# Duo attention with a leaky MoE layer: chunk 0's q in three loads of single tokens, its sinks on GpSimd

## The chip, the core and the metric

The kernel runs on one core of one Trainium2 chip. The metric is the device time of one execution in microseconds (us); the median of five runs counts. The engines are TensorE (PE, with its weight loads as PEld), VectorE (DVE), ScalarE (ACT), GpSimd (POOL) and SyncE (SP). GpSimd, SyncE and ScalarE also issue DMAs, each from its own queue. Only DMAs issued by GpSimd turn float32 into bfloat16 on the way here.

## What is computed

```python
# q, k, v: (4 batches, 8 heads, 768 tokens, 64); heads 0, 2, 6 are "retrieval" heads
scores = q @ k^T / sqrt(64)
causal = rel >= 0                       # rel = query position - key position
stream = causal & (key < 4 | rel < 64)  # 4 sink tokens and a window of 64
a = softmax(where(retrieval head, causal, stream))
x = (a @ v) as (3072 tokens, 512)
h = x @ w_in                            # (512, 2048)
out = max(0.01 * h, h) @ w_out          # (2048, 512), float32 out
```

## The kernel before

**Chunks.** The 3072 tokens are eight chunks of 384 (`CH`): two for each batch, so chunk 0 is the first half of batch 0. Each chunk goes through a preparation (q and k transposed so that the 64 dimensions lie on partitions: tiles `qts` and `kt`), attention (scores, exponential, attention times values into `po`, division, transposition into `xt`), the first layer (`in_slots`, L562, with the leaky function on ScalarE or VectorE) and the second (`out_slots`, L602). The order of every engine's work is written out by hand (`manual_schedule`), the functions return lists of slots that `merge`, `spaced` and `run` interleave, so that the layers of chunk n run beside the attention of chunk n + 1. An instruction waits only for what it needs, but each engine takes its instructions in the order of the program.

**Loads.** GpSimd issues all loads of q, v and the weights and all of k but chunk 0's (`load`, L82; `load_w`, L99). A load of one tensor for one chunk is three DMAs, one for each group `g` of 128 tokens; partition p of group g holds token 128 g + p. At most eight of GpSimd's DMAs are under way; the ninth waits for the first to land. Chunk 0 is the exception: `load_k0` (L70) brings its k as float32 through SyncE in two halves of four heads, and `load_q0` (L78) brings its q in one DMA. Both use the pattern `h (p g) d -> p h (g d)`: partition p holds the tokens 3p, 3p + 1, 3p + 2, so that a piece of three tokens (768 bytes) is contiguous in memory. What comes out of the transposes has then to be put in order of tokens, which `tok` (L331) does by scattered writes.

**The start.** In the program's order:
- GpSimd: the issue for q (L80), `ident` (a memset and a select in masks.py), `m_caus` (L153, L133), three issues for v of chunk 0, w_in parts 0 and 1, then k, q and v of chunk 1, w_in parts 2 and 3, w_out in four parts, and four memsets of `kz`.
- VectorE: memsets of `idle` (what the warm-up matmuls read), `sv`, the ones' column of `va`, `shift`, the zeros in `kt` (L138, L139), `ksink`, two of the five `ats` tiles (L666); `m_h`, a mask of heads, from `ident` (L167, L171).
- ScalarE: five small loads into `sv` (the sink tokens' values), a table load, the other three `ats` tiles (L669).
- `prep_first` (L308): VectorE casts heads 0 to 3 of k (L312), ScalarE heads 4 to 7 (L313). TensorE transposes k in two halves (L324, into banks `pt` and `py`), and between and behind them runs warm-up matmuls, then transposes q (L329) with 24 transposes of 64 columns into two `po` banks. VectorE moves the first half of k into `kt` (L341), makes a mask (L178, L179), and moves the first half of q (L355); ScalarE makes masks (L174, L175), moves the second half of k (L339) and of q (L357).
- Attention of chunk 0: `a0` is a list of slots, each with scores of one group of keys (L416 for retrieval heads, L458 for the others), one slot for the sinks (L396, which reads `ksink` and all of q), and the attention-value matmuls (L383) four slots later. The first four slots need only heads 0 and 2, that is the first half of q. After these four VectorE writes the sink keys out of `kt` into `ksink` (`sink_keys`, two copies, L238), the sink values out of `sv` and `m_h` into `vs` (`sink_values`, L187 and L189), and two 64-column blocks of `ident` into `shift` (`shifts`, L161 and L162). `v_shift_pe` (L218) then multiplies `va` by `shift` on TensorE to get values moved by 64 tokens into `vb` (L224, L227).

`sink_keys` and `sink_values` are also used for later batches, on VectorE; this the change leaves as it is.

Of the kernel before, what the change touches and what calls it, by code (L numbers as in the profile page):

```python
# [12 lines left out]
BF16 = mybir.dt.bfloat16  # L13
ACTF = mybir.ActivationFunctionType
ALU = mybir.AluOpType

IS_RETR = [1, 0, 1, 0, 0, 0, 1, 0]
CH = 384
# [3 lines left out]
def kernel(  # L22
# [12 lines left out]
    nc = tc.nc  # L35
    B, H, S, D = q.shape
    assert (B, H, S, D) == (4, 8, 768, 64)
    NS = int(n_sink)
# [12 lines left out]
    one = ctx.enter_context(tc.tile_pool(name="one", bufs=1))  # L51
# [5 lines left out]
    def bank(tag, shape, dtype):  # L57
        return ps.tile(shape, dtype, name=tag, tag=tag, bufs=BANKS[tag])


    kw, qw = (t[0, :, 0:CH].rearrange("h (p g) d -> p h (g d)", g=3) for t in (k, q))
    nat = {nm: ap.rearrange("b h (c g p) d -> b c p h g d", g=3, p=128) for nm, ap in (("q", q), ("k", k), ("v", v))}
    w_in_r = moe_w_in.rearrange("(g p) n -> p g n", p=128)
    w_out_r = moe_w_out.rearrange("(g p) n -> p g n", p=128)
# [3 lines left out]
    cast = {}  # L68

    def load_k0(half):  # L70
# [3 lines left out]
            cast["k", 0] = rot.tile([128, 3, H, D], BF16, name="kb", tag="kb", bufs=2)  # L74
        hs = slice(4 * half, 4 * half + 4)
        nc.sync.dma_start(out=stage["k"][:, hs], in_=kw[:, hs])

    def load_q0():  # L78
        cast["q", 0] = one.tile([128, H, 3 * D], BF16, name="q0")
        nc.gpsimd.dma_start(out=cast["q", 0][:], in_=qw)  # L80

    def load(n, nms="kqv"):  # L82

        b, c = divmod(n, 2)
        for nm in nms:
            if nm == "k" and n >= BY_DMA:

                for g in range(3):
                    for hh in range(2):
                        nc.gpsimd.dma_start(out=kz[n % 2][:, g, hh::2, D * hh : D * hh + D],  # L90
                                            in_=nat[nm][b, c, :, hh::2, g])
                continue
            if nm != "v":
                cast[nm, n] = rot.tile([128, 3, H, D], BF16, name=f"{nm}b", tag=f"{nm}b", bufs=2)
            for g in range(3):
                o = va[b % 2][:, 3 * c + g, :, 0:D] if nm == "v" else cast[nm, n][:, g]
                nc.gpsimd.dma_start(out=o, in_=nat[nm][b, c, :, :, g])  # L97

    def load_w(which, i):  # L99

        if which == "in":
            c = slice(512 * i, 512 * i + 512)
            nc.gpsimd.dma_start(out=w_in_bf[:, :, c], in_=w_in_r[:, :, c])
        else:
            c = slice(4 * i, 4 * i + 4)
            nc.gpsimd.dma_start(out=w_out_bf[:, c, :], in_=w_out_r[:, c, :])
# [5 lines left out]
    def bf(name, *shape):  # L112
        return one.tile([128, *shape], BF16, name=name)

    ident = bf("ident", 128)
# [3 lines left out]
    kt = [bf(f"kt{i}", 4, 2, S) for i in range(2)]  # L119
    va = [bf(f"va{i}", 6, H, D + 1) for i in range(2)]  # L120
    vb = [bf(f"vb{i}", 5, H, D + 1) for i in range(2)]
    vs = [bf(f"vs{i}", H, D + 1) for i in range(2)]

    sv = one.tile([128, B, D], FP32, name="sv")
# [21 lines left out]
    m_h = bf("m_h", H)  # L146
# [9 lines left out]
    def spread(ap, n, w):  # L156
        return ap.rearrange("p (o r) -> p o r", o=1).to_broadcast([128, n, w])

    def shifts():

        nc.vector.tensor_copy(shift[:, 0, 0:64], ident[:, 64:128])  # L161
        nc.vector.tensor_copy(shift[:, 1, 64:128], ident[:, 0:64])  # L162

    def masks_sinks():

        with nc.allow_low_precision("one term of each sum is not zero"):
            nc.vector.tensor_reduce(m_h[:], ident[:, 0 : NS * H].rearrange("p (h r) -> p h r", r=NS),  # L167
                                    axis=mybir.AxisListType.X, op=ALU.add)
        for h in range(H):
            if IS_RETR[h]:  # L170
                nc.vector.memset(m_h[:, h : h + 1], 0.0)  # L171
# [11 lines left out]
        nc.vector.tensor_copy(m_win0[:, 0, :], m_caus[:, 0:64])  # L183
        nc.vector.memset(m_win0[0:NS, 1, :], 1.0)

    def sink_values(b):
        nc.vector.tensor_copy(vs[b % 2][:, :, D], m_h[:])  # L187
        m = m_h[:, 1:H].rearrange("p (h o) -> p h o", o=1).to_broadcast([128, H - 1, D])
        nc.vector.tensor_tensor(vs[b % 2][:, 1:H, 0:D], spread(sv[:, b, :], H - 1, D), m, op=ALU.mult)  # L189


    idle = {}
# [1 line left out]
    def warm_up(n, w=128):  # L194
        if not idle:
            idle["s"] = bf("idle", 512)
            nc.vector.memset(idle["s"][:], 0.0)
            idle["d"] = bank("psS", [128, 512], FP32)
        for _ in range(n):
            nc.tensor.matmul(idle["d"][:, 0:w], lhsT=idle["s"][:, 0:128], rhs=idle["s"][:, 0:w], start=True, stop=True)  # L200
# [7 lines left out]
    qts = {}  # L208
# [17 lines left out]
            src = p[:, 0:w].rearrange("p (h d) -> p h d", h=7)  # L226
            nc.vector.tensor_copy(vb[0][:, t, 1:H, :], src)  # L227

    def sink_keys(n):
        b, c = divmod(n, 2)  # L230
        if c:
            return
        for hh in range(2):
            r = slice(64 * hh, 64 * hh + 64)
            d = ksink[b % 2].rearrange("p (a c) -> p a c", a=4)[r, :, NS * hh : NS * hh + NS]
            st = [p for p in range(4) if not IS_RETR[2 * p + hh]]
            for ps2 in [slice(0, 4)] if len(st) == 4 else [slice(p, p + 1) for p in st]:
                nc.vector.tensor_copy(d[:, ps2], kt[b % 2][r, ps2, hh, 0:NS])  # L238

    def prep_pair(n, p, tag="pt", eng=("v", "v", "v")):  # L240
        b, c = divmod(n, 2)
# [66 lines left out]
    def prep_first():  # L308

        k0 = stage["k"].rearrange("p h (g d) -> p g h d", g=3)  # L310
        qts[0] = rot.tile([128, 4, CH], BF16, name="qt", tag="qt", bufs=3)
        nc.vector.tensor_copy(cast["k", 0][:, :, 0:4], k0[:, :, 0:4])  # L312
        nc.scalar.activation(out=cast["k", 0][:, :, 4:8], in_=k0[:, :, 4:8], func=ACTF.Copy)  # L313
        pts = {}
        for nm, half, tag in (("k", 0, "pt"), ("k", 1, "py"), ("q", 0, "po"), ("q", 1, "po")):
            pt = pts[nm, half] = bank(tag, [128, 2, 4, 128], BF16)
            if nm == "q":
                continue
            if half == 1:
                warm_up(9)  # L320
            for e in range(2):
                p = 2 * half + e
                for g in range(3):
                    nc.tensor.transpose(pt[:, e, g, :], cast[nm, 0][:, g, 2 * p : 2 * p + 2, :], ident[:])  # L324
        warm_up(8)
        for p in range(4):
            for g in range(3):
                for hh in range(2):
                    nc.tensor.transpose(pts["q", p // 2][64 * hh : 64 * hh + 64, p % 2, g, :],  # L329
                                        cast["q", 0][:, 2 * p + hh, D * g : D * g + D], ident[:])  # L330
        tok = lambda ap: ap.rearrange("p e (t g) -> p e t g", g=3)  # L331

        def k_rows(half, hh, act=False):
            ps2 = slice(2 * half, 2 * half + 2)
            r = slice(64 * hh, 64 * hh + 64)
            src = pts["k", half][r, :, 0:3, :].rearrange("p e g t -> p e t g")
            dst = tok(kt[0][r, ps2, hh, 0:CH])
            if act:
                nc.scalar.activation(out=dst, in_=src, func=ACTF.Copy)  # L339
            else:  # L340
                nc.vector.tensor_copy(dst, src)  # L341

        def q_rows(half):
            return (tok(qts[0][:, 2 * half : 2 * half + 2, :]),
                    pts["q", half][:, :, 0:3, :].rearrange("p e g t -> p e t g"))

        nc.vector.tensor_sub(m_w[:], m_caus[:, 64:128], m_caus[:, 0:64])
        negative_causal()
        k_rows(0, 0)
        k_rows(0, 1)  # L350
        k_rows(1, 0, True)
        k_rows(1, 1, True)
        negative_window()
        d, r = q_rows(0)
        nc.vector.tensor_copy(d, r)  # L355
        d, r = q_rows(1)
        nc.scalar.activation(out=d, in_=r, func=ACTF.Copy)  # L357

# [262 lines left out]
    def run(*lists):  # L621
        for l in lists:
            for f in l:
                f()
# [16 lines left out]
        return [lambda p=p: prep_pair(n, p) for p in range(4)]  # L641


    load_q0()
    make_identity(nc, ident)
    warm_up(9, 512)
    nc.vector.memset(sv[:], 0.0)
# [9 lines left out]
    load(0, "v")  # L657
    load_w("in", 0)
    load_w("in", 1)
    load(1, "kq")  # L660
    load(1, "v")
    load_w("in", 2)
    load_w("in", 3)
    for j, a in enumerate(ats):
        if j < 2:
            nc.vector.memset(a[:, :, 1:3, :], 0.0)  # L666
        else:
            z = idle["s"][:, 0:CH].rearrange("p (a e t) -> p a e t", a=3, e=2)
            nc.scalar.activation(out=a[:, :, 1:3, :], in_=z, func=ACTF.Copy)  # L669
    masks_sinks()  # L670
    for i in range(4):
        load_w("out", i)
    for t in kz:
        nc.gpsimd.memset(t[:, :, 0::2, D:], 0.0)
        nc.gpsimd.memset(t[:, :, 1::2, 0:D], 0.0)
    prep_first()
    A0 = Attention(0, ("psS", "ph"), po_tags=("po", "po", "py", "po"))
    a0 = A0.slots(order=[0, 2, 1, 3, 4, 5, 6, 7], lag=lambda t: 4, XLAG=None, sink_after={0, 2})
    warm_up(8)
    run(a0[0:4])  # L680
    sink_keys(0)
    sink_values(0)
    shifts()
    run(a0[4:6])
    v_shift_pe()
    run(a0[6:14])
    i0 = in_first(0, ("ph", "psS", "ph", "psS"))
# [36 lines left out]
    m = merge(out0[5:] + out_slots(1, ("ph", "py", "ph")), a2)  # L724
# [63 lines left out]
```

## Time and profile before

| what | us |
|---|---|
| median of five runs (lowest, highest) | 237.37 (236.95, 237.73) |
| the profiled execution | 237.08 |
| its span, first to last instruction | 235.4 |
| TensorE busy | 227.9 (97%) |
| ScalarE busy | 129.3 (55%) |
| VectorE busy | 89.7 (38%) |
| GpSimd busy | 77.8 (33%) |
| granted TensorE clock, mean | 0.998 |
| first score matmul (L416) | 9.76 after the span's start |

The profile is of one execution on the chip. Its page gives busy time by engine, the span in 40 slices, the chain of waits that ended last, and groups of instructions by source line. Each row of the chain names a start, a length, and what took that time: an engine with tile and line, or "issue" where the engine waited for nothing that the profile shows. In the timeline a row is a start, the time from there to the end of the last of `xcount` instructions, engine, line and tiles (output <- input); in brackets stands idle time ahead of it and what ended that. The last columns of a row of groups are busy time and mean ns of one, then idle time ahead. Matmuls are pipelined, so one that shows 0.3 us may be followed by the next after half of that. For DMAs the profile has packets by queue (the software queue is the one that GpSimd fills) and the time from an issue to its landing.

### The profile page before, as it was taken

The page shows a single profiled execution, that of the slowest core. Times are in us where ns is not written, and L with a number is a line of the kernel's source. Part 1 is how long each engine was busy: PE and PEld are TensorE (multiplying, and loading weights), DVE is VectorE, ACT ScalarE, POOL GpSimd, SP SyncE. Part 2 cuts the span into 40 slices and gives each one's busy share as a digit, 9 for nine tenths or more (in the row PEclk, how much of TensorE's full clock was granted, in tenths as well). Part 3 has the DMA queues.
Part 4 walks back from the last instruction along what each step waited for, and adds up shares of the span by engine and source line. Part 5 has one row for each costly group of instructions (what it writes and reads, how often), then busy time and mean ns, then how long its engine had stood idle before and what let it go on. Part 6 is the DMA issues. An engine that isn't in the chain of part 4 may idle for free.

```text
span 235.4 us, 5134 instructions
## 1 busy us (share of the span) xinstructions
PE 227.9 (97%) x2064; PEld 138.9 (59%) x2064; DVE 89.7 (38%) x244; ACT 129.3 (55%) x282; POOL 77.8 (33%) x102
## 2 busy tenths in 40 slices
PE   7899899999999999999999999999999999999994
PEld 2786566556664676666546665566556665555553
DVE  7875479208662254144212351344213341111121
ACT  4977775661540798666357763556366763333300
POOL 7938942879762274372049100000000000000000
PEclk9999999999999999999999999999999999999999
DMA  7999999999999999999999998495210221111112
GB/s 168 178 180 163 220 222 186 155 124 167 143 162 223 166 189 159 158 115 169 150 199 178 128 140 150 111 137 154 72 45 0 65 58 40 45 45 45 47 45 89
DMA packets 110699, 30.54 MB, mean 130 GB/s; under 512 B 101460, under 2 KB 106836, under 8 KB 110676
## 3 DMA queue, kind: packets, MB, share of 16 engines
q0 software_dynamic: 74144, 13.24, 76.9%
q1 hardware_dynamic: 36432, 16.95, 39.0%
q8 instruction: 16, 0.26, 0.5%
q14 instruction: 7, 0.06, 0.1%
q10 hardware_dynamic: 100, 0.02, 0.0%
HBM read 27.28 MB, written 6.29 MB: 143 GB/s over the span
## 4 chain that ended last, share of the span: by engine, by line
PE 86%; DVE 5%; DMA 4%; ACT 3%; issue 1%; ACTq 0%
PE ph L562 26%; PE py L602 14%; PE pt L602 10%; PE po L383 7%; PE psS L562 6%; PE ph L602 4%; PE psS L416 4%; PE psS L602 4%; DMA xt<-xs 4%; PE psS L458 2%; ACT at L425 2%; PE po L602 1%; PE psS L396 1%; PE ph L416 1%; DVE kt L341 1%
## 5 line engine op out<-in xcount | busy, mean ns | idle before, releaser
L562 PE MATMUL ph<-xt,w_in_bf 128*128 128x384 bf16 x416 | 85.7, 326 | 0.6 <-DMA xt<-xs 0.5
L570 ACT ACTIVATE g<-ph 128x384 bf16<-128x384 f32 x102 | 50.1, 491 | 51.6 <-PE ph L562 51.2
L562 PEld LDWEIGHTS <-w_in_bf 128*128 128x128 bf16 x512 | 46.5, 98 | 31.4 <-issue 0.5
L602 PEld LDWEIGHTS <-g 128*128 128x128 bf16 x400 | 35.8, 98 | 26.3
L602 PE MATMUL py<-w_out_bf,g 128*128 128x512 bf16 (+1 forms) x176 | 44.6, 369 | 0.0
L425 ACT ACTIVATE at<-psS 128x384 bf16<-128x384 f32 x66 | 32.4, 495 | 11.6 <-PE psS L416 10.2
L90 POOL DMA_DIRECT2D kz<-in_k_dram x30 | 22.4, 766 | 29.6 <-DVE kz L736 12.3
L602 PE MATMUL pt<-w_out_bf,g 128*128 128x512 bf16 x112 | 30.2, 379 | 0.0
L97 POOL DMA_DIRECT2D va<-in_v_dram x24 | 21.2, 898 | 9.8 <-DMA w_in_bf<-in_moe_w_in_dram 3.6
L97 POOL DMA_DIRECT2D qb<-in_q_dram x21 | 18.7, 906 | 10.9 <-DMA va<-in_v_dram 4.9
L416 PE MATMUL psS<-qt,kt 128*128 128x384 bf16 (+2 forms) x86 | 21.5, 288 | 0.2
L562 PE MATMUL psS<-xt,w_in_bf 128*128 128x384 bf16 x96 | 20.5, 326 | 0.0
L383 PE MATMUL po<-va,at 128*128 128x65 bf16 x237 | 19.5, 193 | 0.2 <-DVE at L433 0.2
L383 PEld LDWEIGHTS <-at 128*128 128x128 bf16 x252 | 15.9, 98 | 5.6 <-issue 0.6
L466 ACT ACTIVATE ats<-psS 128x384 bf16<-128x384 f32 x32 | 15.8, 492 | 4.9 <-PE psS L458 4.3
L607 DVE COPY o<-py 128x512 f32<-128x512 f32 (+1 forms) x11 | 7.3, 664 | 28.1 <-PE py L602 28.1
L501 DVE TENSOR_TENSOR xs<-po,linv 128x384 bf16<-128x384 f32 x30 | 16.7, 557 | 1.0
L416 PEld LDWEIGHTS <-kt 128*128 128x128 bf16 x108 | 10.2, 97 | 8.7 <-issue 1.5
L458 PEld LDWEIGHTS <-kt 128*128 128x128 bf16 x240 | 11.8, 98 | 5.5 <-issue 0.2
L433 DVE TENSOR_TENSOR at<-at,m_caus 128x128 bf16<-128x128 bf16 x21 | 4.7, 224 | 26.0 <-ACT at L425 25.9
L383 PEld LDWEIGHTS <-ats 128*128 128x128 bf16 x240 | 11.4, 97 | 3.8 <-DVE ats L476 0.6
L570 ACT ACTIVATE g<-psS 128x384 bf16<-128x384 f32 x22 | 10.8, 491 | 4.7 <-PE psS L562 4.7
(135 smaller groups left out, 243.2 us busy)
## 6 DMA issues: line engine op xcount, KB each, us to landing
out_dram<-o SPq DMA_DIRECT2D x23, 256.0 KB, 2.9
va<-in_v_dram POOLq DMA_DIRECT2D x24, 128.0 KB, 10.9
qb<-in_q_dram POOLq DMA_DIRECT2D x21, 128.0 KB, 10.7
w_in_bf<-in_moe_w_in_dram POOLq DMA_DIRECT2D x4, 512.0 KB, 9.2
w_out_bf<-in_moe_w_out_dram POOLq DMA_DIRECT2D x4, 512.0 KB, 14.7
kz<-in_k_dram POOLq DMA_DIRECT2D x30, 64.0 KB, 7.8
vb<-va SPq DMA_DIRECT2D x8, 195.0 KB, 6.5
vb<-va SPq DMA_DIRECT2D x6, 130.0 KB, 8.3
```

The costliest lines, as they stand in the source:

```text
L90: nc.gpsimd.dma_start(out=kz[n % 2][:, g, hh::2, D * hh : D * hh + D], in_=nat[nm][b, c, :, hh::2, g])
L97: nc.gpsimd.dma_start(out=o, in_=nat[nm][b, c, :, :, g])
L383: nc.tensor.matmul(o, lhsT=lhsT, rhs=rhs, start=first, stop=False, skip_group_check=True)
L416: nc.tensor.matmul(s[:, off : off + w], lhsT=kt[i][:, p, hh, 128 * kj : 128 * kj + 128], rhs=qts[n][:, p, lo:CH], start=(j == 0), stop=(j ...
L425: nc.scalar.activation(out=a[:, 0:off], in_=s[:, 0:off], func=ACTF.Exp, scale=SM)
L458: nc.tensor.matmul(s[:, 64 * m : 64 * m + 64], lhsT=kt[i][:, p, hh, k0 : k0 + 128], rhs=qts[n][:, p, 64 * m : 64 * m + 64], start=(m == 0) ...
L466: nc.scalar.activation(out=av_, in_=s[:, 0:CH].rearrange("p (j e f) -> p j e f", j=3, e=2), func=ACTF.Exp, scale=SM)
L501: nc.vector.tensor_tensor(xs[:], po[:, :, :, 0:D], linv.to_broadcast([128, 3, 2, D]), op=ALU.mult)
L562: nc.tensor.matmul(ph[:, 0:CH], lhsT=w_in_bf[:, g, 128 * t : 128 * t + 128], rhs=xts[n][:, g, :], start=(g == 0), stop=(g == KG - 1))
L570: nc.scalar.activation(out=gs[n][:, t, :], in_=ph[:, 0:CH], func=ACTF.Prelu, alpha=0.01)
L602: nc.tensor.matmul(py[n][:, 0 : c1 - c0], lhsT=gs[n][:, ng, 128 * tt : 128 * tt + 128], rhs=w_out_bf[:, ng, c0:c1], start=(ng == 0), stop= ...
L607: nc.vector.tensor_copy(o[:, 0 : c1 - c0], py[n][:, 0 : c1 - c0])
```

## The change

Chunk 0's q is loaded as every other chunk's: three DMAs of 128 tokens each, one token and head (256 bytes) to a piece, into a tile `qb`. q's tokens are then in their natural order after the transposes, which are 12 of 128 columns, grouped by g with two warm-up matmuls ahead of the second and the third group; the moves into `qts` write contiguously. k of chunk 0 stays in its interleaved order.

The sink keys and values of chunk 0 are written by GpSimd instead of VectorE. In GpSimd's order they stand behind the issues of v of chunk 0 and w_in parts 0 and 1, and ahead of all loads of chunk 1. The keys' copies wait for `kt`, which VectorE and ScalarE write; the values' product waits for the loads into `sv`. `shifts` moves ahead of `prep_first`, so on VectorE ahead of the cast of k. A third `ats` tile is zeroed by VectorE, so ScalarE zeroes two.

```diff
-    def load_q0():
-        cast["q", 0] = one.tile([128, H, 3 * D], BF16, name="q0")
-        nc.gpsimd.dma_start(out=cast["q", 0][:], in_=qw)
...
-    def sink_values(b):
-        nc.vector.tensor_copy(vs[b % 2][:, :, D], m_h[:])
+    def sink_values(b, eng=None):
+        eng = eng or nc.vector
+        eng.tensor_copy(vs[b % 2][:, :, D], m_h[:])
         m = m_h[:, 1:H].rearrange("p (h o) -> p h o", o=1).to_broadcast([128, H - 1, D])
-        nc.vector.tensor_tensor(vs[b % 2][:, 1:H, 0:D], spread(sv[:, b, :], H - 1, D), m, op=ALU.mult)
+        eng.tensor_tensor(vs[b % 2][:, 1:H, 0:D], spread(sv[:, b, :], H - 1, D), m, op=ALU.mult)
...
-    def sink_keys(n):
+    def sink_keys(n, eng=None):
...
-                nc.vector.tensor_copy(d[:, ps2], kt[b % 2][r, ps2, hh, 0:NS])
+                (eng or nc.vector).tensor_copy(d[:, ps2], kt[b % 2][r, ps2, hh, 0:NS])
...
         warm_up(8)
-        for p in range(4):
-            for g in range(3):
-                for hh in range(2):
-                    nc.tensor.transpose(pts["q", p // 2][64 * hh : 64 * hh + 64, p % 2, g, :],
-                                        cast["q", 0][:, 2 * p + hh, D * g : D * g + D], ident[:])
+        for g in range(3):
+            warm_up(2 if g else 0)
+            for p in range(4):
+                nc.tensor.transpose(pts["q", p // 2][:, p % 2, g, :], cast["q", 0][:, g, 2 * p : 2 * p + 2, :], ident[:])
...
         def q_rows(half):
-            return (tok(qts[0][:, 2 * half : 2 * half + 2, :]),
-                    pts["q", half][:, :, 0:3, :].rearrange("p e g t -> p e t g"))
+            return (qts[0][:, 2 * half : 2 * half + 2, :].rearrange("p e (g t) -> p e g t", g=3),
+                    pts["q", half][:, :, 0:3, :])
...
-    load_q0()
+    load(0, "q")
     make_identity(nc, ident)
...
     load_w("in", 0)
     load_w("in", 1)
-    load(1, "kq")
-    load(1, "v")
-    load_w("in", 2)
-    load_w("in", 3)
     for j, a in enumerate(ats):
-        if j < 2:
+        if j < 3:
...
     masks_sinks()
+    shifts()
+    prep_first()
+    sink_keys(0, nc.gpsimd)
+    sink_values(0, nc.gpsimd)
+    load(1, "kqv")
+    load_w("in", 2)
+    load_w("in", 3)
     for i in range(4):
         load_w("out", i)
...
-    prep_first()
     A0 = Attention(0, ("psS", "ph"), po_tags=("po", "po", "py", "po"))
...
     warm_up(8)
-    run(a0[0:4])
-    sink_keys(0)
-    sink_values(0)
-    shifts()
-    run(a0[4:6])
+    run(a0[0:6])
     v_shift_pe()
```

Line numbers named for the kernel before are those of its listing above; in the changed kernel the same places stand a few lines higher (its L351 is L355 of before, its L93 is L97).

## Prediction

> **What bounds the kernel.** I read the shares of busy time first, then the chain of waits, then the first 26 us engine by engine in the timeline, because every edit acts there. The page's first rows:
>
> ```profile
> PE 227.9 (97%) x2064; PEld 138.9 (59%) x2064; DVE 89.7 (38%) x244; ACT 129.3 (55%) x282; POOL 77.8 (33%) x102
> PEclk9999999999999999999999999999999999999999
> PE 86%; DVE 5%; DMA 4%; ACT 3%; issue 1%; ACTq 0%
> ```
>
> TensorE is busy 97% at its full granted clock, so a gain must come from a place where it waits. The change touches one: the start. The chain that ended last, cut to 4 to 10 us, runs there almost wholly on VectorE:
>
> ```profile
> 4.52 0.05 DVE m_h L167
> 4.57 0.06 issue
> 4.63 1.06 DVE kb L312
> 5.68 0.05 issue
> 5.73 0.52 PE pt L324 x6
> ...
> 7.26 0.97 DVE kt L341
> ...
> 8.75 0.97 DVE qt L355
> 9.71 0.04 issue
> 9.76 0.32 PE ph L416
> ```
>
> From 9.76 to 19.2 us the same chain is TensorE without a gap. So the moment of the first score matmul counts, and after it whether a load arrives later than TensorE wants it. GpSimd's timeline shows the issue queue that is edited:
>
> ```profile
> 1.32 1.01 POOL L80 DMA_DIRECT2D q<-in_q_dram  x1 [0.81 <-POOLq L769]
> 2.33 0.23 POOL masks.py:197 MEMSET ident<- 128x128 bf16 x1
> 2.63 0.29 POOL masks.py:199 TENSOR_SCALAR_AFFINE_SELECT ident<-ident 128x128 bf16<-128x128 bf16 x1
> ...
> 3.37 2.66 POOL L97 DMA_DIRECT2D va<-in_v_dram  x3
> 6.00 1.52 POOL L103 DMA_DIRECT2D w_in_bf<-in_moe_w_in_dram  x2
> 7.48 2.68 POOL L97 DMA_DIRECT2D kb<-in_k_dram  x3
> ```
>
> **Part 1, three issues for q.** Three issues of this size take 2.63 us from start to next start (3.37 to 6.00), one of the old took 1.01: all behind it on GpSimd moves by 1.6 us, or 1.75 if the first of them takes 1.01 too. `ident` is then ready at 4.55 to 4.67 instead of 2.92, v0's issues start at 5.0 to 5.12, the two w_in issues end at 9.15 to 9.27 instead of 7.52. VectorE's first use of `ident` (the reduction L167, at 4.45) moves to 4.65 anyway by part 3, so the delay of `ident` is covered, by 0.1 us at most.
>
> **Part 2, q's bytes.** The DMA view in windows of 1 us gives the software queue's rate, packets and MB. At 5 to 6 us it carries the old q (768 bytes read, 384 written), at 8 to 9 us v0 (256 read, 128 written):
>
> ```profile
> q0 software_dynamic: 476, 0.18, 154.8%
> q0 software_dynamic: 1213, 0.15, 240.1%
> ```
>
> The old q is 1024 packets; at 476 and 574 per us (the next window) they take 1.95 us. The new is 3072 packets like v0's; at 1213 per us 2.53 us, so 0.58 later. The old landed 6.4 us after its issue, at 7.73, while the transposes L329 started at 7.80. The last third of the new lands at about 8.3 (8.0 to 8.6). By the Trainium skill (DMA: Bandwidth & Descriptors, Specifications) transfers under 512 bytes fall off the line rate; if that meant half the rate, q would land near 9.7 and this change would lose a microsecond on that alone. These two rows show a loss of a sixth only, so the rows decide.
>
> The first third can be transposed while the last is on its way. TensorE's own work is 12 transposes of 128 columns (0.056 each, six in 0.34 on the chain) and 4 warm-ups (0.069), 0.95, against 0.86 for 24 narrow ones. VectorE wants q at 8.75. With the last four transposes after 8.35 (0.06 each, 0.16 to the end) half 0 is there at 8.65 to 8.75: just covered; the cover is gone if q lands after 8.45.
>
> **Part 3, VectorE's chain.** A third `ats` memset is put ahead of the cast (two take 0.41 now: +0.21), and so are the two `shift` copies (0.085 apart at 10.99 and 11.08: +0.17). The cast L312 would start at 5.0. What it then takes is the open term. VectorE's rows show that its copies from SBUF to SBUF stall beside GpSimd's DMA issues:
>
> ```profile
> L312 DVE CAST kb<-f 128x768 bf16<-128x768 f32 x1 | 1.0, 1047 | 0.1
> L187 DVE COPY vs<-m_h 128x8 bf16<-128x8 bf16 x1 | 0.7, 665 | 0.0
> L238 DVE COPY ksink<-kt 64x4 bf16<-64x4 bf16 x1 | 0.5, 526 | 0.0
> L238 DVE COPY ksink<-kt 64x16 bf16<-64x16 bf16 x1 | 0.2, 169 | 0.0
> ```
>
> A copy of 4 columns took 526 ns and one of 16 took 169; L187 takes 177 later in the kernel. The slow ones began 0.3 to 0.4 us after an issue's start and finished as it ended (10.15 and 11.04); L162, 0.13 us after an issue's start, ran in 175. The cast began 0.35 us into v0's second issue. Rows with 768 columns that can't collide, since they read PSUM, take 955 with scattered writes (L341) and 555 with contiguous ones (L278), so of 1047 between 0.1 and 0.5 was stall. In the new order GpSimd is at `m_caus` or at v0's first issue when the cast starts. Bounds: 0.5 shorter, or 0.9 longer if the issue is taken for itself first (wait to 5.9 to 6.0, 0.6 to run). I take about 0.35 shorter, because 5.0 to 5.2 lies ahead of or within 0.15 us of that issue's start, nearest to the row L162. The cast then ends at about 5.7: no change.
>
> The evacuation of q by VectorE becomes contiguous: 957 to 555, **-0.40**. ScalarE's half is not faster (0.81 scattered; 0.49 for 384 columns gives the same). ScalarE loses one `ats` copy (0.45), its cast L313 can start when k's second half has landed (1.30 + 4.4 = 5.7 instead of 6.02); that is off the chain but lets q's transposes begin earlier. Sum up to the first score matmul: 0.38 - 0.35 - 0.40 = -0.37, so 9.4.
>
> **Part 4, what is late next.** v0 queues behind q's 0.58. Its last third was issued at 5.14 and landed 5.9 later, at 11.0; the second group of attention-value matmuls needs it at 11.61 on TensorE's timeline. It lands at 11.4 to 11.6 now, and is wanted at 11.25: a wait of 0.15 to 0.35. So of 0.37 about **0.15** is left, and TensorE hands that on, as it is busy from there to 19 us.
>
> **Part 5, sinks on GpSimd.** VectorE loses four operations (9.62 to 11.08); it next waits for TensorE 1.0 us at 12.29, so this gains nothing. On GpSimd they wait for `kt` (ScalarE's last rows, 9.0) and for the issues ahead, so start at 9.2. GpSimd has no such rows; its smallest memset took 98 ns, 128 columns of the select 292, so the four cost between 0.7 (VectorE's 620 for 448 columns and three at the floor) and 1.6 us (448 columns at the select's pace); I take 1.2. The keys' two copies are done by 9.7, and TensorE wants them at 10.4 (10.74 now). The operands of L189 arrive long before (0.02 MB). Queued behind are chunk 1's k, q, v: first issue 10.4 to 10.9 instead of 7.48. Its packets would in any case wait for the weights ahead: kb landed 10.4 to 10.6 us after its issues (17.9 to 19.8), 9 us of it in the queue. They move by the queue's 0.5, to 20.4, against 21.03 for the first transpose of kb; qb goes from 22.6 to 23.1 against 23.67. Margins of 0.5: covered, with little to spare. Sum for the whole: **-0.15 us**.
>
> The profiled execution took 237.08 (235.4 of span, 1.7 around it); the median of the five runs is 237.37. The change is added to the median: **237.2**.
>
> **The rivals.**
> - *The cast falls into the issue* (slower). If `ident`'s delay lets VectorE's copies wait for the select of `m_caus` (4.85 to 5.15), the cast comes 0.2 to 0.4 us after v0's issue started and waits for its end, as L238 did. It ends at 6.55, +0.85; with -0.40 on q the first score is 0.45 later, and v0 no longer waits: +0.5, **237.9**. It decides from a cast start of about 5.25. For it: L187 and L238; against it: L162 and the 0.1 us that has to be lost first. By the Trainium skill (SBUF — State Buffer, SBUF: two separate sides) the one that starts first has the shared pair for its whole instruction; by it the select or the issue wins and the loss would be 0.65; row L162 shows a copy running inside an issue.
> - *Loads late.* If v0's packets can start only 2.3 us after their issue's end, as q's did (issued by 2.33, first packets at 4.6), v0's last third lands near 11.9, and kb and qb follow, each past its margin: +0.7, **238.0**. Against it: behind q the queue is never seen empty.
> - *The whole gain.* The cast loses its full 0.5 of stall and v0 comes in time: -0.5, **236.9**.
> - *Nothing reaches the end*, because DMA transposes hold TensorE at 122 us (0.5 us there): 237.4, within the forecast.
>
> **How the numbers follow.** Forecast, with the last rival, 0.41; cast in the issue 0.29; loads late 0.18; whole gain 0.12. About 0.2% (0.47 us) is what a measurement of this kernel can tell. The forecast is within it, of the cast's case 0.05 and of the late loads 0.02: same 0.48, slower 0.40, faster 0.12. The range takes in the whole gain, the cast's case and the milder half of late loads: 236.8 to 238.1.
>
> **What would show it.** Right: L351 (q by VectorE) at 0.56; the cast below 0.75 us, from 5.0 to 5.2; first score at 9.3 to 9.5; a wait of TensorE near 11.3 on `va`; kb's transposes without a wait. The cast's rival: that row above 1 us, first score after 10.1. Late loads: TensorE idle at 11.5 or 21 with a DMA as releaser. Wrong altogether: a difference that arises behind 30 us.

## The result, and the profile after

The changed kernel takes **238.24 us** (median of 44 runs) against 237.43 for the kernel before (79 runs on the same chips). Three of the 44 ran in a slower state; the other 41 have a median of 238.11, and the ratio is made from these. It is 1.0028, with a 95% interval of 1.0016 to 1.0039: some 0.7 us **slower**. I had forecast 237.2 with a range of 236.8 to 238.1. The profiled execution took 237.78 us with a span of 236.1, against 237.08 and 235.4 before, so it shows the loss: 0.7.

The shares of busy time and of the chain, of the page of the changed kernel:

```profile
PE 229.4 (97%) x2056; PEld 140.8 (60%) x2056; DVE 87.5 (37%) x241; ACT 129.0 (55%) x281; POOL 81.2 (34%) x108
PEclk9999999999999999999999999999999999999998
...
PE 87%; DVE 4%; DMA 3%; ACT 3%; issue 1%; ACTq 0%
```

They show nothing of it: TensorE is busy 97% as before. The chain cut to 4 to 11.5 us answers to the one shown of before (columns: start, duration, work):

```profile
4.73 0.17 DVE m_h L163
...
5.31 0.60 DVE kb L309
5.91 0.05 issue
5.96 0.82 PE pt L321 x6
6.78 0.96 PE psS L197 x9
7.74 0.64 PE py L321 x6
8.38 0.85 PE psS L197 x8
9.23 0.39 PE po L326 x4
...
10.07 0.13 PE po L326 x2
10.20 0.02 issue
10.22 0.57 DVE qt L351
10.79 0.04 issue
10.83 0.32 PE ph L412
```

The first score starts at 10.83, 1.07 later than before (9.76), and not at 9.4. VectorE did what was worked out. q's thirds landed at 7.44, 8.37 and 9.27, the whole q of before at 7.75. But in this chain TensorE stands still for none of them. From 5.96 on it works without a gap, until 9.5 at half pace (though the granted clock is shown as 1.00 there): six transposes took 0.82 where the kernel before's took 0.51. So its transposes of q came late, the last four 0.64 after their load had landed. The first and the last four in its timeline:

```profile
9.03 0.60 PE L326 MATMUL po<-ident,qb 128*128 128x128 bf16 x4
9.91 0.39 PE L326 MATMUL po<-ident,qb 128*128 128x128 bf16 x4
```

In two of the runs below (e2, i2) TensorE does wait for q's last third, and the first score comes 0.98 behind its landing. By that the landing at 9.27 alone would give 10.25; so of the 1.07 about 0.5 is the landing and 0.6 the pace, as an estimate. GpSimd's timeline:

```profile
1.32 2.77 POOL L93 DMA_DIRECT2D qb<-in_q_dram  x3 [0.81 <-POOLq L763]
...
5.13 2.74 POOL L93 DMA_DIRECT2D va<-in_v_dram  x3
7.84 1.53 POOL L99 DMA_DIRECT2D w_in_bf<-in_moe_w_in_dram  x2
9.32 0.25 POOL L235 COPY ksink<-kt 64x4 bf16<-64x4 bf16 x1
10.17 0.20 POOL L235 COPY ksink<-kt 64x16 bf16<-64x16 bf16 x1 [0.60 <-POOL ksink L235]
10.43 0.22 POOL L184 COPY vs<-m_h 128x8 bf16<-128x8 bf16 x1
10.63 0.94 POOL L186 TENSOR_TENSOR vs<-sv,m_h 128x448 bf16<-128x448 f32 x1
11.52 2.71 POOL L93 DMA_DIRECT2D kb<-in_k_dram  x3
```

The four sink operations take 1.6 us together, and chunk 1's issues start at 11.52 instead of 7.48.

That looks like a story of 1.07 us at the start. It is not the whole one. If both traces are laid side by side, TensorE runs 1.08 us behind up to 120 us, and from the first `g` of chunk 4 (the first output of the leaky function there; at 122.85 before, 123.56 after) to the end only 0.71 behind. Something at 122 us took up 0.37, or it set the end by itself. The chain there, of the kernel before and of the changed one:

```profile
113.41 0.57 DVE xs L501
113.97 0.02 issue
113.99 8.40 DMA xt<-xs
122.39 0.04 issue
```

```profile
114.49 0.57 DVE xs L497
115.06 0.02 issue
115.08 8.02 DMA xt<-xs
123.10 0.04 issue
```

This is the fourth DMA transpose of chunk 4's attention output: issued by SP when VectorE has `xs`, landed 8 us later. TensorE waits for it in both, 0.5 us before and about 0.3 after. In the changed kernel it also left 1.09 later, because `xs` waits for TensorE's attention; so by this pair alone a late start could have delayed it. Two chains meet at 122 us, that of TensorE and that of the loads, and the experiments have to say which of them the change made longer.

**The theories.** *The start:* q lands later, and the late first score reaches the end, less what the wait at 122 us takes up. *The clock:* TensorE's half pace at the start makes it late. *The other edits:* sinks on GpSimd, the third `ats`, the later issues of chunk 1. These three went into the first four runs, where the texts call them Q (q's late landing), C and S. The first four runs left none of the three standing and brought up another, *the queue:* q's 2048 more pieces make every later load late, and TensorE waits for a load, or for this `xt`, wherever it comes early; the start matters only if it is later still. In the texts from the fifth run on, **Q stands for the queue and S for the start**.

### The profile page after: what moved, and what is told of

Same layout as the page of the kernel before. It is cut to its first block, busy times and chain, and to the rows that moved or that the text cites. A ratio compares the mean times of both kernels' runs of the same rounds, so it can differ in the third digit from the quotient of the medians.

```text
span 236.1 us, 5125 instructions
## 1 busy us (share of the span) xinstructions
PE 229.4 (97%) x2056; PEld 140.8 (60%) x2056; DVE 87.5 (37%) x241; ACT 129.0 (55%) x281; POOL 81.2 (34%) x108
## 4 chain that ended last, share of the span: by engine, by line
PE 87%; DVE 4%; DMA 3%; ACT 3%; issue 1%; ACTq 0%
PE ph L558 26%; PE py L598 14%; PE pt L598 10%; PE po L379 7%; PE psS L558 6%; PE ph L598 4%; PE psS L412 4%; PE psS L598 4%; DMA xt<-xs 3%; PE psS L454 2%; ACT at L421 2%; PE po L598 1%; PE psS L392 1%; PE ph L412 1%; PE psS L197 1%
## 5 line engine op out<-in xcount | busy, mean ns | idle before, releaser
L93 POOL DMA_DIRECT2D qb<-in_q_dram x24 | 21.3, 900 | 12.3 <-DMA va<-in_v_dram 4.9
L93 POOL DMA_DIRECT2D va<-in_v_dram x24 | 21.3, 906 | 7.4 <-DMA w_out_bf<-in_moe_w_out_dram 3.7
```

## The experiments

Each kernel was timed in 12 runs beside 29 to 35 of the kernel before on the same chip. Single executions of one kernel lie up to 3 us apart, so the medians tell 0.7 from nothing, but hardly 0.3. The profiled executions decide more.

**1. The loss sits in q's three loads.** Two kernels: the changed one with q in one load as before (with its narrow transposes and scattered moves), and the kernel before with nothing but q's three loads.

```diff
# e1_q_one, against the changed kernel     # e2_q_three, against before: the same, reversed
-    load(0, "q")
+    load_q0()
```

> The changed kernel with chunk 0's q in one load of three tokens again (24 narrow transposes, scattered moves); sinks on GpSimd, shift copies and the third ats tile on VectorE stay. Theory Q (the late landing of q's last third, 9.27 us instead of 7.75, is the loss): the whole loss goes, 237.4 or up to 0.3 less. Theory C (TensorE's pause ahead of its first transposes, 0.68 us instead of 0.45, lets its full pace begin one window later, at 9.5 instead of 5.7): the pause stays at 0.5 to 0.7, since VectorE still has two copies and a memset ahead of the cast, so half of the loss or more stays, 237.8 to 238.2. Theory S (the other edits, sinks on GpSimd above all, are the loss): all of it stays, 238.1.

> The kernel before with only q's three loads (with their 12 transposes and contiguous moves); sinks, shift copies and ats tiles as before. Theory Q: first score at 10.1 to 10.3, loss 0.4 to 0.7, so 237.9 to 238.1. Theory C: the cast waits 0.1 to 0.3 for ident, the pause grows little, loss 0 to 0.3 beyond what theory Q gives. Theory S: 237.4, no loss.

Measured: 237.48, ratio 1.0000 (0.9971 to 1.0029), with one load; 238.53, ratio 1.0054 (1.0029 to 1.0079), with three loads alone. So the three loads alone bring the loss. The sinks on GpSimd, the third `ats`, the order of `shift` and of chunk 1's issues show no cost, though the first interval is as wide as the loss itself. But the traces contradict the start: with three loads alone the first score came at 9.63, earlier than before, and the execution was still 0.84 longer in span; TensorE waited 0.57 us for a part of w_in at 29.7 us and 0.60 for `xt` at 123. With one load it came at 11.14 (q landed at 9.52 in that execution), 1.38 late, and the median is that of before.

**2. The pace of TensorE at the start.** Two 512-wide warm-up matmuls more in the changed kernel, two fewer in the kernel before.

```diff
# e3_warm11, changed kernel                # e4_before_warm7, kernel before
-    warm_up(9, 512)                       -    warm_up(9, 512)
+    warm_up(11, 512)                      +    warm_up(7, 512)
```

> The changed kernel with 11 warm-up matmuls of 512 columns instead of 9 ahead of the first transposes; at 0.427 us each they end at 6.1 and close the pause. Theory C: full pace from 5 to 8 us in every run, 0.3 to 0.6 less than the changed kernel (237.5 to 237.9), first score at 10.1 to 10.3, which is what q's landing still sets. Theory Q alone: 238.2, unchanged, as q's last third lands at 9.3 in either case. Theory S: unchanged.

> The kernel before with 7 warm-up matmuls of 512 columns instead of 9: the pause ahead of the first transposes grows from 0.45 to 1.3 us, nothing else changes. Theory C: the first transposes run at half pace, full pace begins after 8 us in most runs, first score at 10.2 to 10.8, 0.4 to 0.9 slower (237.8 to 238.3). Theories Q and S: 237.4, unchanged.

Measured: 238.18, ratio 1.0032 (1.0006 to 1.0059), and 237.82, ratio 1.0032 (1.0001 to 1.0064). With 11 warm-ups TensorE transposed q at full pace, the first score of the profiled execution was at 9.82, and the loss stayed: the half pace falls as the cause. From 100 us on TensorE waited 1.1 us for `xt`. The kernel with fewer warm-ups came out where the clock's theory had put it (237.8 to 238.3), by an interval that hardly clears 1. But in its profiled execution the first six transposes took 0.51, full pace, and the late first score (11.10) is q's landing at 9.47. Why it costs something stays open.

**3. Pieces and start apart.** Two loads that nobody needs, without any change of the start; and a late start, without any change of a load.

```diff
# f1_extra_load, against before, behind w_in part 1
+    extra = one.tile([128, 2, H, D], BF16, name="extra")
+    for g in range(2):
+        nc.gpsimd.dma_start(out=extra[:, g], in_=nat["v"][0, 1, :, :, g])
# f2_start_late, against before, ahead of the first score
     warm_up(8)
+    warm_up(5, 512)
```

> The kernel before with two further loads of 1024 pieces of 256 bytes (from v, into a tile that nothing reads) between w_in's first half and chunk 1's loads; the start is untouched. Theory Q (q's three loads make the software queue's stream late, by 1.2 to 1.5 us at its 16384th packet in the profiles of the kernels with three loads, and TensorE waits for a load, or for a transpose queued behind loads, wherever it comes early): the stream is about 1.7 us late (2048 pieces at 1213 per us), TensorE waits on a DMA somewhere between 20 and 123 us, +0.6 to +1.2 us, 238.0 to 238.6. Theory S (what counts is the moment of the first score matmul): first score as before, 0 +- 0.2.

> The kernel before with five more 512-wide warm-up matmuls ahead of the first score: TensorE starts about 1.07 us later, no load is changed. Theory S: the 1.07 go through up to 118 us, 0.35 to 0.5 of them are taken up by the wait for DMA transposes at 122 us, the end is 0.6 to 0.7 later: 238.1. Theory Q in its strict form (the loads' stream alone sets the end): 0 to +0.3. If both lateness of loads and lateness of the start cost about the same each by itself, they do not add: the end is the later of the two.

Measured: 238.07, ratio 1.0027 (0.9996 to 1.0058), and 238.44, ratio 1.0026 (1.0000 to 1.0051). Neither interval is clear of 1 by itself. The traces, one of each, show where the time went. TensorE's waits between 10 and 130 us with the extra loads, and the place in its timeline (the last bracket is the idle time before the row and what ended it):

```profile
PE ph L562 <- DMA xt<-xs: 1.2, 1, 1.2
```

```profile
121.54 0.65 PE L562 MATMUL ph<-xt,w_in_bf 128*128 128x384 bf16 x3
123.41 0.32 PE L562 MATMUL ph<-xt,w_in_bf 128*128 128x384 bf16 x1 [1.22 <-DMA xt<-xs]
```

The first score was 0.23 later than before; the first `g` of chunk 4 0.98 later. 2048 pieces that nobody reads, issued at 7.5 us, hold TensorE up at 122 us. With the late start the same wait is gone and the first `g` of chunk 4 is 0.88 later by TensorE's own lateness. So both chains are there, and each can cost about the same; in these executions the later one counts, and they do not add. One thing is not told apart, here and below: wherever 2048 pieces are added or given back, two loads are added or given back with them.

**4. Giving pieces back.** Chunk 1's k in one load of three-token pieces, 2048 fewer. Its transposes are left as they were, so chunk 1's keys are not the reference's.

```diff
# f3_three_k1_one, against e2_q_three; f4_before_k1_one, against before; j3_after_k1_one, changed kernel
-    load(1, "kq")
+    load_k1()          # k[0, :, CH : 2 * CH] by "h (p g) d -> p h (g d)", one DMA
+    load(1, "q")
```

> The kernel with q's three loads alone, and chunk 1's k in one load of 1024 pieces of 768 bytes instead of three of 256 bytes (its tokens then stand in another order and are transposed as before, so that chunk 1's keys are not the reference's; work and instructions of TensorE are the same). That gives the queue back what q's three loads cost it, from chunk 1's k on. Theory Q: the waits on loads behind 22 us go, 0.4 to 1.0 us faster than with q's three loads alone (238.53): 237.5 to 238.1. Theory S: 238.5, unchanged.

> The kernel before with chunk 1's k in one load of three-token pieces (as in the run beside it, chunk 1's keys in another order). Theory Q: the stream is about 1 us earlier than before; if loads hold TensorE in the kernel before too, 0.2 to 0.5 faster, 236.9 to 237.2; if they do not, 237.4. Theory S: 237.4.

> The changed kernel with chunk 1's k in one load alone, in the same way. Theory Q: 237.4 to 237.9, as q's three loads alone with the same (237.92). A cost of the three loads apart from their pieces: 238.2.

Measured: 237.92, ratio 1.0011 (0.9983 to 1.0039); 237.49, ratio 0.9994 (0.9971 to 1.0017); 237.79, ratio 1.0020 (0.9993 to 1.0047). The medians of both kernels with three loads come down, by 0.6 and 0.45, and the kernel before gains nothing, as the queue has it; but the intervals overlap those of the kernels without this edit, so the gain is not shown. And not all comes back: the profiled execution of j3 still waited 0.7 for `xt` at 122 us and 0.9 for chunk 3's q at 78.

**5. The transposes at 122 us out of the loads' way.** Chunk 6's v is loaded behind chunk 4's attention, as chunk 7's loads are in both kernels. That leaves q's three loads as they are, and takes away their consequence.

```diff
# h1_before_v6, h2_after_v6 (changed kernel), h3_three_v6 (e2), h4_one_v6 (e1)
             if n == 4:
 
+                nc.vector.memset(va[1][0:1, 0:3, 0, 0:1], 0.0)
+                load(6, "v")
                 nc.vector.memset(kz[(n + 3) % 2][0:1, 0, 0, 0:1], 0.0)
-            load(n + 3)
+            load(n + 3, "kq" if n == 3 else "kqv")
```

> The kernel before with chunk 6's v loaded behind chunk 4's attention, as chunk 7's loads are already (its three issues leave 105 to 109 us and come at about 121), so that 3072 pieces less share the DMA engines with chunk 4's four xt transposes. Theory Q: the wait for xt at 122 us (0.5 in the profile) goes, 0 to 0.5 faster, 237.0 to 237.4, and g number 68 starts 112.45 behind the first score matmul, as in the kernels that do not wait there. Theory S: the same, as it allows for this wait too. A rival to the edit itself: the shift of chunk 6's v comes late on SP and chunk 5's xt behind it; then a new wait on a DMA at 140 to 150 us and a slower kernel.

> The changed kernel with the same edit. Theory Q (the loss is TensorE's wait for xt at 122 us, or the same delay taken earlier at a load): with nothing late at 122 the loss goes, 237.0 to 237.6, within 0.3 of the kernel before with this edit. Theory S (the loss is the late first score, as q's last third lands late): it stays 0.7 behind the kernel before with this edit, 237.9 to 238.2.

> q's three loads alone, with the same edit. Theory Q: 0.5 to 1.0 us faster than q's three loads alone (238.53), 237.3 to 238.0; waits for chunk 1's loads at 22 to 30 us may stay. Theory S: unchanged, 238.5.

> The changed kernel with q in one load, and the same edit. Theory Q: as the kernel before with this edit, 237.0 to 237.4, and no more than 0.3 ahead of the changed kernel with it. Theory S: 0.7 ahead of the changed kernel with it.

Measured: 237.39, ratio 1.0002 (0.9976 to 1.0027); **237.34**, ratio 0.9998 (0.9981 to 1.0015); **237.19**, ratio 1.0005 (0.9985 to 1.0024); 237.75, ratio 1.0017 (0.9999 to 1.0035). The changed kernel loses its whole loss (238.24 to 237.34; its interval ends at 1.0015, just short of the 1.0016 at which the one without the edit begins), and so does the kernel with three loads alone (238.53 to 237.19, intervals clearly apart). The one with q in a single load stands behind the one with three, where the start wanted it 0.7 ahead. The late start falls as the cause of the loss.

What the queues did in the 16.5 us from 106 on is seen in the DMA view, first the kernel before, then the same kernel with the edit (columns: packets, MB, time of the packets as a share):

```profile
q0 software_dynamic: 7270, 0.91, 105.9%
q1 hardware_dynamic: 3915, 1.85, 71.0%
```

```profile
q1 hardware_dynamic: 3635, 1.92, 65.4%
q0 software_dynamic: 3907, 0.49, 49.3%
```

With 3363 packets fewer in GpSimd's queue, the fourth `xt` landed 4.2 us after its issue (114.10 to 118.31) instead of 8.4. By the Trainium skill (DMA: Bandwidth & Descriptors, Queues, rings and completion order) each DMA engine takes the queues it has work for in turn, packet by packet, so a transpose has to share with a backlog of loads; this pair of rows agrees. The chain in that place is then TensorE alone (changed kernel with the edit):

```profile
119.99 0.65 PE ph L558 x4
120.64 0.16 PE psS L412
120.80 0.65 PE pt L598 x3
121.45 0.16 PE psS L412
121.61 0.65 PE ph L558 x4
```

**6. What is left.** Both reliefs together. In the first three runs k's order was kept by narrow transposes and scattered moves, in the last two it was not.

```diff
# i1_before_v6_k1, i2_after_v6_k1, i3_after_k1: prep_two for k of chunk 1
+                        nc.tensor.transpose(pt[64 * hh : 64 * hh + 64, e, g, :],
+                                            cast[nm, n][:, 2 * p + hh, D * g : D * g + D], ident[:])
...
+                nc.vector.tensor_copy(kt[...].rearrange("p e (t g) -> p e t g", g=3), pt[r, :, 0:3, :].rearrange("p e g t -> p e t g"))
# j1_before_both (h1), j2_after_both (h2): load_k1 as in 4, nothing else
```

> The kernel before with chunk 6's v behind chunk 4's attention and chunk 1's k in one load of three-token pieces, taken apart by narrow transposes and scattered moves as chunk 0's q is (the keys are the reference's). If the rest of the spread is late loads: 236.7 to 237.0, faster than before. If it is the start (q's landing differs by up to 2 us between executions and nothing is left that takes a late start up): 237.3 to 237.4.

> The changed kernel with both. Late loads: 236.7 to 237.1. The start: 237.2 to 237.4, as without chunk 1's part (237.34).

> The changed kernel with chunk 1's k in one load alone; chunk 6's v where it was. Theory Q: the queue gets back 2048 pieces, the number that q's three loads add: 237.4 to 237.9, as q's three loads alone with the same (237.92). Theory S, or any cost of the three loads apart from their pieces: 238.2.

> The kernel before with chunk 6's v behind chunk 4's attention, and chunk 1's k in one load of three-token pieces that are transposed and moved as before (chunk 1's keys in another order, not the reference's). If what is left is late loads: 236.6 to 237.0. If it is the spread of the start: 237.2 to 237.4.

> The changed kernel with both, in the same way. Late loads: 236.6 to 237.0; the start: 237.2 to 237.4.

Measured: 238.91, 238.84 and 238.94 for the three; 238.04, ratio 1.0014 (0.9986 to 1.0043), and 237.05, ratio 1.0000 (0.9980 to 1.0021), for the two. The three answer nothing, and all my figures for them were wrong: I had forgotten the price of their own edit. Chunk 1's moves, 556 ns with contiguous writes in the changed kernel, became

```profile
L291 DVE COPY kt<-py x2: 950/955/960, 22.0 to 22.9; 64x768 bf16<-64x768 bf16 x2
L291 DVE COPY kt<-pt x2: 949/954/960, 23.9 to 24.9; 64x768 bf16<-64x768 bf16 x2
```

and TensorE waits 1.0 us for them: 1.4 us in all on its chain. Of the two, the changed kernel with both reliefs has the lowest median of all, but not by more than can be told from no change, and the kernel before with both is not faster. No version was shown to beat the kernel before. What spreads single executions from 236.4 to 239 was not settled; the start is one part of it, as the profiles show: over ten executions each, q landed at 7.51 to 9.87 us with one load (median 8.86) and its last third at 8.57 to 9.50 with three (median 8.74).

**The whole in one table.** From the first score to the first `g` of chunk 4 it takes 112.46 us if no load holds TensorE (f2 and h2 show it: 11.28 to 123.73, 9.89 to 122.36), and that `g` starts 0.46 behind the landing of the fourth `xt` where TensorE waits for it (before, f1: 122.39 to 122.85, 123.37 to 123.83). The later of the two is what each profiled execution of this table has, but for j2, where 0.22 more, lost ahead of 33 us, stay open; most spans end 112.5 behind it. Left out are i1 and i2, which paid 1.4 for their narrow transposes, and j1, of which more at the end:

| kernel | first score | + 112.46 | `xt` landed | + 0.46 | first `g` of chunk 4 | span | median |
|---|---|---|---|---|---|---|---|
| before | 9.76 | 122.22 | 122.39 | **122.85** | 122.85 | 235.4 | 237.43 |
| changed | 10.83 | 123.29 | 123.10 | **123.56** | 123.56 | 236.1 | 238.24 |
| e1, q in one load | 11.14 | **123.60** | 121.64 | 122.10 | 123.60 | 236.1 | 237.48 |
| e2, three loads alone | 9.63 | 122.09 | 123.24 | **123.70** | 123.70 | 236.2 | 238.53 |
| e3, 11 warm-ups | 9.82 | 122.28 | 123.49 | **123.95** | 123.95 | 236.5 | 238.18 |
| e4, 7 warm-ups | 11.10 | **123.56** | 121.99 | 122.45 | 123.56 | 236.1 | 237.82 |
| f1, extra loads | 9.99 | 122.45 | 123.37 | **123.83** | 123.83 | 236.3 | 238.07 |
| f2, late start | 11.28 | **123.74** | 120.47 | 120.93 | 123.73 | 236.2 | 238.44 |
| f3, e2 and k1 in one | 9.79 | 122.25 | 122.56 | **123.02** | 123.02 | 235.6 | 237.92 |
| f4, before and k1 in one | 10.82 | **123.28** | 120.94 | 121.40 | 123.28 | 235.8 | 237.49 |
| h1, before and v6 late | 9.84 | **122.30** | 118.31 | 118.77 | 122.32 | 235.0 | 237.39 |
| h2, changed and v6 late | 9.89 | **122.35** | 121.15 | 121.61 | 122.36 | 234.9 | 237.34 |
| h3, e2 and v6 late | 9.72 | 122.18 | 122.70 | **123.16** | 123.16 | 236.0 | 237.19 |
| h4, e1 and v6 late | 9.99 | **122.45** | 118.02 | 118.48 | 122.46 | 235.2 | 237.75 |
| i3, changed and k1 taken apart | 9.87 | 122.33 | 123.45 | **123.91** | 123.92 | 236.4 | 238.94 |
| j2, changed and both | 9.64 | **122.10** | 120.41 | 120.87 | 122.32 | 235.0 | 237.05 |
| j3, changed and k1 in one | 9.76 | 122.22 | 123.89 | **124.35** | 124.35 | 236.9 | 237.79 |

Where q came in one load and no other load was changed (before, e1, e4, f2), the transpose landed at 122.39 at the latest; with three loads and nothing given back (changed, e2, e3) at 123.10 at the earliest. The start varies in both, and it does not make this difference: issued at 115.06 to 115.52, the transpose landed at 120.47 to 121.99 in f4, e4, e1 and f2, and in the changed kernel, issued at 115.08, at 123.10. Against the queue speaks that the changed kernel's `xt` landed late also where pieces were given back: at 123.45 in i3 and 123.89 in j3.

The late loads reach this transpose by a second road too, which no run varied by itself. SP takes its DMAs in order, and ahead of chunk 4's `xt` stand transposes of a later chunk's q, which wait for their loads. SP stood 6.3 us for such a load in the changed kernel, 8.0 in e2 (the rows below), 6.9 in e3 and 6.6 in the kernel before; in e1, e4, f2 and f4 no wait of SP for a load between 84 and 105 us was longer than 2.3. The first of chunk 4's four `xt` left at 108.0 to 110.6 in the one group and at 105.8 to 106.4 in the other. So the profiled execution of the kernel before is itself one with late loads.

```profile
SPq L301 <- DMA qb<-in_q_dram: 6.3, 1, 6.3
...
SPq L304 <- DMA qb<-in_q_dram: 8.0, 1, 8.0
```

In h3's execution SP issued that transpose at 116.39, 2.3 later than in h1, so the edit did not take the wait away each time.

## Why the prediction was wrong

- **Held.** The cast escaped the issue: it is 676 ns instead of 1047, 0.37 less where I took 0.35. q's evacuation by VectorE is 557 ns. `ident`'s delay is covered. These rows of VectorE in 4 to 13 us show both:

```profile
L309 DVE CAST kb<-f 128x768 bf16<-128x768 f32 x1 | 0.7, 676 | 0.0
...
L351 DVE COPY qt<-po 128x768 bf16<-128x768 bf16 x1 | 0.6, 557 | 1.0 <-PE po L326 1.0
```

- **Part 2, "The last third of the new lands at about 8.3 (8.0 to 8.6)":** too early. It landed between 8.57 and 9.50 in ten executions. The packets were as worked out: the last one started at 7.46 to 7.60, against 6.86 to 7.14 for the old load, near the 0.58 of the sum (the rate was 1120 per us at 6 to 7 us, not 1213). What the sum had too small is the time from there to the landing, 1.1 to 1.9. The 1.0 us of idle time in the row above is this and the half pace. But I also measured it against one profile of before, whose q had landed at 7.75, the second earliest of ten. Against the usual landing the three loads lose nothing, and with three loads the first score mostly came at 9.6 to 9.9 (in eight of ten executions; 10.83 is the latest). So 9.4 was 0.2 to 0.5 too early as a rule, and 1.4 in the execution profiled.
- **Part 4, the wait for v0 near 11.3:** it did not come, with the first score at 9.63 (e2) either.
- **Part 5, the sinks:** 1.6 us, my upper bound, hidden as I said. kb landed at 19.07 to 20.87, and TensorE wanted it at 22.1.
- **The step that failed: "They move by the queue's 0.5 ... covered, with little to spare".** First, its size. Counted in the order of start, the last packet of w_in's two loads starts at 14.50 to 14.98 us in the ten traces with one load, and at 15.78 to 16.39 in the ten with three: 1.4 later, not 0.5. Of this 0.6 is q's own; the first w_in load alone took 2.64 to 3.06 us instead of 1.83 to 2.40, and why is open (it is issued 1.8 us later, and that was not varied by itself). Second, its end. I followed the delay to the next two tiles, found 0.5 us of cover in each, and stopped. But the page has the DMA engines at 9 tenths or more in every slice of 5.9 us from 6 to 141 us (finer slices show a dip of about 1 us at 115 in the kernel before), so there is little that could take the delay up. Counted over the same loads and without packets of 4 bytes, the 52000th packet of GpSimd's queue starts at 97.56 before and 99.56 after, 2.0 later (95.7 to 97.6 in the six traces with one load and no piece added or given back, 98.7 to 101.5 in the five with three). The late loads then stand in front of the transposes of chunk 4, and the term that the sum had at nothing, TensorE's wait for a load or an `xt` far behind 30 us, is where the 0.7 came from.
- **The rival "Nothing reaches the end", put at 237.4 "within the forecast".** It names the right place and takes it as fixed. A wait for a DMA is not a wall at 122 us that only takes up changes of TensorE; it is the end of another chain, which this change made longer, by 0.7 from one profiled execution to the other. The sign given for "wrong altogether", a difference that arises behind 30 us, is what came. A first score at 9.4 would hardly have helped: in e2 it came at 9.63, and the first `g` of chunk 4 at 123.70.
- **What the start did cost.** By the table, in the profiled execution the late start alone would have given 123.29, +0.44; the `xt`, as it landed, gave 123.56, +0.71, and set the end.

## What to carry to other kernels

A wait for a DMA late in the kernel, even one of half a microsecond, means that the loads' chain and the engine's chain end together there. While the DMA engines are busy nearly throughout, loads added far ahead can move that wait (here 2048 pieces more at 2 us, and an `xt` 0.7 to 1.1 us later at 122), and have to be followed up to it and not only to the next tile that is loaded. And the start of one profiled execution is one draw: before 0.4 us are worked out from when a load landed, see how far that landing differs between executions.

## What the hardware showed that was not expected

- **The landing of the first load.** One DMA of 1024 pieces, issued at 1.32 to 1.33 us, landed between 7.51 and 9.87 us in ten profiled executions, though its last packet started between 6.86 and 7.14 in all of them. So the landing of a load is not told by the starts of its packets.
- **The clock was halved after a short idle time.** In the profiled execution of j1 (240.62 us, its kernel's median is 238.04) q landed at 9.87, and TensorE's granted clock fell. The rows by window (TensorE's busy time first, the granted clock behind POOL):

```profile
8.00:10.00 2.00, 0.08 (x3) 0.09 (x5) 0.62 (x3) 1.03 (x2) 1.29 (x2) 1.00 2.13 166
10.00:11.50 1.50, 1.34 (x33) 1.12 (x34) 1.02 (x2) 0.68 (x1) 1.34 (x2) 1.00 1.37 197
11.50:14.90 3.40, 3.40 (x26) 2.65 (x26) 1.45 (x6) 2.41 (x6) 2.15 (x3) 0.50 1.27 204
14.90:17.00 2.10, 2.10 (x36) 1.48 (x34) 1.17 (x2) 1.12 (x3) 0.87 (x1) 1.00 1.64 192
```

  TensorE waited 2.08 us for q; 1.6 us after it had begun again, it got half the clock for 3.4 us, while it was busy throughout. The first `g` of chunk 0 was 3.36 late, 1.73 by the first score and 1.63 by the clock. By the Trainium skill (TensorE: Matmul & The Clock Gate, Part 1: The HAM clock gate) the clock is set by windows of about 3.4 us that run freely; the 3.4 us agree, but the page has the clock fall after an idle window, and here it was busy for some 1.4 us of the 3.4 before the fall. Waits of 1.84 us (e1) and 1.70 us (e4) at the same place were not followed by a fall. That the idle time is the cause is likely, but was not tested.
- **VectorE's scattered writes** of 64 x 768 cost 955 ns against 556, at chunk 1 as at chunk 0.
